# Banded attention and a two-projection feed-forward net on one core: the operands of both projections moved to fixed places modulo 128 bytes

## The chip, the cores and the metric

The kernel runs on one core of one Trainium2 chip. The metric is the device time of one execution in microseconds (us); lower is better. Three executions of the kernel before took 661.93, 663.27 and 664.57 us, so the median is 663.27 us.

## The reference: what is computed

Eight heads of attention over four sequences of 768 positions with head size 64, with a linear bias by distance and a mask that keeps a band of 96 positions and 8 global ones, and behind it a net with one hidden layer of 2048 and a leaky gate, on 3072 rows of 512.

```python
# q, k, v: (4, 8, 768, 64)
scores = q @ k.T / 8 + bias            # bias = -slope[head] * distance
scores = where(is_global | is_local, scores, -1e9)   # n_global = 8, n_local = 96
a = softmax(scores)
x = (a @ v) as rows of 8 * 64          # 3072 x 512
h = x @ w_in                           # 512 x 2048
g = maximum(0.01 * h, h)
out = g @ w_out                        # 2048 x 512
```

## The kernel before

**Two paths.** `fast_path` computes all under the assumption that the band holds (few global positions, a short band). At the end `band_holds` (line 756) looks whether it did, and only if not a general path (`general_attention`, `general_ffn`) computes everything again. With the inputs here the general path is skipped.

**Work units.** The 3072 rows are 24 steps of 128 rows. The attention of a step is two units of four heads, so there are 48 units, each handled in an "event" (line 348): scores (line 192), biased scores on VectorE (line 206), exponentials on ScalarE (line 219), sums, a transposition (by TensorE for the first 14 units, line 278, by VectorE and DMA for the others, lines 250 and 223), the product with v (line 324), and a split of the resulting x into a rounded part `xh` and a rest `xl` (lines 345 and 346).

**The projections.** To keep float32 precision, each operand is kept as two fp32r tiles, a rounded high part and a low rest (`wih`/`wil` for w_in, `woh`/`wol` for w_out, `xh`/`xl`, `gh`/`gl`), and each product is three matmuls: high by high, high by low, low by high. In the first projection the weights are stationary and x moves (lines 891 to 893 for the first two chunks of 384 rows, line 449 for the nine chunks of 256 rows); in the second one the gated hidden values `gh`/`gl` are stationary and the weights move, 512 wide (lines 912 to 914, and line 493). The text below calls a run of first-projection matmuls an **H group** (24 matmuls of 256 columns at line 449; 12 of 384 before that) and a run of the second an **O group** (12 matmuls of 512 columns, 9 of them in the early part).

**Eight pairs to a chunk.** A chunk of 256 rows goes through eight pairs of hidden blocks, `p` = 0 to 7. In each step `s` of the last loop (line 631) stand first the attention events that are due, then the H group of step `s`, its gate (line 453), and the O group of step `s - 2`. Eight of the nine such chunks multiply the last three pairs (`p` = 5, 6, 7) with seven products instead of eight half products, from precomputed sums of weight blocks (`prepare`, line 537, tiles `h5` to `h7` and `l5` to `l7`); such an O group has 21 matmuls, nearly all 256 columns wide; in pair 5 two of them are 512 wide. `prepare` also overwrites a quarter of `woh` and `wol` for these pairs (line 568).

**Order.** TensorE's matmuls are kept in the order of the program, and nearly all of ScalarE's and VectorE's instructions too.

**Where tiles lie.** Tiles are placed in pools one behind the other, so that the size of a tile shifts all later ones in its pool and in the pools behind it, while pools with `side="right"` are placed from the other end of the memory and do not shift. The pool `keep` (line 922) holds the weights; behind it come `const`, `raw` (q, k, v), `att`, and then `ffn`, `kept_rows` and `x0`, which are given back to be used by `a` (`gh`, `gl`), `ev` and `w` (`h5` ...). The pools `x1`, `x2` (`xh`, `xl` of the later chunks), `t` and `pt` (`pt_d`) are on the right side. A tile `gap` of 16 floats ahead of the sums in `prepare` (line 542) already shifts these by 64 bytes.

Of the kernel before, what the change touches and what calls it, by code (L numbers as in the profile page):

```python
# [10 lines left out]
F32 = mybir.dt.float32  # L11
F32R = mybir.dt.float32r
BF16 = mybir.dt.bfloat16
I32 = mybir.dt.int32
I64 = mybir.dt.int64
# [3 lines left out]
P = 128  # L19
# [13 lines left out]
FAST = 3  # L33
# [18 lines left out]
def fast_path(ctx, tc, qp, kp, vp, wi, wo, nvec, weights, nmall, out, B, H, S):  # L52
    nc = tc.nc
    NB = S // P
    DM = H * D
    NK = DM // P
    NF = wi.shape[0]
# [7 lines left out]
    wih, wil, woh, wol = weights  # L65
# [5 lines left out]
    ffn = later.enter_context(tc.tile_pool(name="ffn", bufs=2))  # L71
    kept_rows = later.enter_context(tc.tile_pool(name="kept_rows", bufs=1))
    xts = {0: later.enter_context(tc.tile_pool(name="x0", bufs=1))}
    edge = ctx.enter_context(tc.tile_pool(name="edge", bufs=1, side="right")).tile([P, EDGE], F32, name="edge")
    nc.gpsimd.memset(edge, 0.0)
    stage = early.enter_context(tc.tile_pool(name="stage", bufs=STAGES, side="right"))
# [572 lines left out]
def split_float64(tc, pin, pool, raw, dh, dl):  # L649

    nc = tc.nc
    w2 = raw.bitcast(I32).rearrange("p (n two) -> p n two", two=2)
    lo, hi = w2[:, :, 0], w2[:, :, 1]
    w = pool.tile([P, lo.shape[1]], F32, tag="work", name="w32", bufs=2)
    wb = w.bitcast(I32)
    w3 = w.rearrange("p (a b) -> p a b", a=dh.shape[1]) if len(dh.shape) == 3 else w

    def scale():  # L660
        pin(nc.scalar.activation(out=w, in_=hi.bitcast(F32), func=AF.Copy, scale=2.0 ** -112))

    def shift():
        pin(nc.vector.tensor_scalar(out=wb, in0=wb, scalar1=3, scalar2=0x7FFFFFF8,
                                    op0=ALU.logical_shift_left, op1=ALU.bitwise_and))
        pin(nc.vector.scalar_tensor_tensor(out=wb, in0=hi, scalar=-0x80000000, in1=wb,
                                           op0=ALU.bitwise_and, op1=ALU.bitwise_or))

    def low():
        pin(nc.vector.scalar_tensor_tensor(out=wb, in0=lo, scalar=29, in1=wb,  # L670
                                           op0=ALU.logical_shift_right, op1=ALU.bitwise_or))

    def high():
        pin(nc.scalar.copy(out=dh, in_=w3))

    def rest():
        pin(nc.vector.tensor_tensor(out=dl, in0=w3, in1=dh.bitcast(F32), op=ALU.subtract))

    return scale, shift, low, high, rest
# [172 lines left out]
                    nc.sync.dma_start(out=dst.rearrange("o d s -> (o d) s"), in_=xo)  # L852


def general_ffn(tc, weights, xs, out):
    nc = tc.nc
    wih, wil, woh, wol = weights
    NK, NF, DM = wih.shape[1], woh.shape[1], woh.shape[2]
    CT = xs.shape[-1]
    with ExitStack() as ctx:  # L860
        work = ctx.enter_context(tc.tile_pool(name="hwork", bufs=2))
        ps_h = ctx.enter_context(tc.tile_pool(name="hps", bufs=2, space=bass.MemoryType.PSUM))
        ps_o = ctx.enter_context(tc.tile_pool(name="hpo", bufs=1, space=bass.MemoryType.PSUM))
        xv = xs.rearrange("b j p k t -> (b j) p k t")
        ov = out.rearrange("(c p) m -> c p m", p=CT)
        with tc.For_i(0, xv.shape[0], 1) as c:
            x = work.tile([P, NK, CT], F32, name="hx", bufs=1)
            xh = work.tile([P, NK, CT], F32R, name="hxh", bufs=1)
            xl = work.tile([P, NK, CT], F32R, name="hxl", bufs=1)
            nc.sync.dma_start(out=x, in_=xv[bass.ds(c, 1)].rearrange("o p k t -> (o p) k t"))  # L870
            nc.scalar.copy(out=xh, in_=x)
            nc.vector.tensor_tensor(out=xl, in0=x, in1=xh.bitcast(F32), op=ALU.subtract)
            o = ps_o.tile([P, CT // P, DM], F32, name="hpo")
            for f in range(NF):
                gh, gl = hidden(tc, lambda ins: None, work, ps_h, weights, xh, xl, f, CT)
                for tt in range(CT // P):
                    project(tc, o[:, tt, :], weights, gh, gl, tt, f, f == 0, f == NF - 1)
            ob = work.tile([P, CT // P, DM], F32, name="hob")
            nc.scalar.copy(out=ob, in_=o)
            nc.sync.dma_start(out=ov[bass.ds(c, 1)].rearrange("o (t p) m -> p (o t) m", p=P), in_=ob)  # L880


def hidden(tc, pin, pool, psum, weights, xh, xl, f, CT, *steps):

    nc = tc.nc
    wih, wil = weights[:2]
    NK = wih.shape[1]
    fs = slice(f * P, (f + 1) * P)
    ps = psum.tile([P, CT], F32, tag="ps_h", name="ps_h")
    for k in range(NK):  # L890
        tc.keep_in_program_order(nc.tensor.matmul(ps, lhsT=wih[:, k, fs], rhs=xh[:, k, :CT], start=(k == 0), stop=False))
        tc.keep_in_program_order(nc.tensor.matmul(ps, lhsT=wih[:, k, fs], rhs=xl[:, k, :CT], start=False, stop=False))
        tc.keep_in_program_order(nc.tensor.matmul(ps, lhsT=wil[:, k, fs], rhs=xh[:, k, :CT], start=False, stop=(k == NK - 1)))
    t = pool.tile([P, CT], F32, name="t")
    pin(nc.scalar.copy(out=t, in_=ps))
    pin(nc.vector.scalar_tensor_tensor(out=t, in0=t, scalar=0.01, in1=t, op0=ALU.mult, op1=ALU.max))
    gh = pool.tile([P, CT], F32R, name="gh")
    gl = pool.tile([P, CT], F32R, name="gl")
    if steps:
        steps[0]()  # L900
    pin(nc.scalar.copy(out=gh, in_=t))
    pin(nc.vector.tensor_tensor(out=gl, in0=t, in1=gh.bitcast(F32), op=ALU.subtract))
    if steps:
        steps[1]()
    return gh, gl
# [11 lines left out]
def tile_kernel(tc, a, out, B, H, S):  # L917
    nc = tc.nc
    NF, _, NK, _ = a["wi"].shape
    DM = a["wo"].shape[3]  # L920
    NB = S // P
    with tc.tile_pool(name="keep", bufs=1) as keep, tc.tile_pool(name="xs", bufs=1, space=bass.MemoryType.DRAM) as dram:
        nvec = read_counts(tc, keep, a["ngl"])
        nmall = keep.tile([P, B * NB * H], F32, name="nmall")
        weights = (keep.tile([P, NK, NF * P], F32R, name="wih"), keep.tile([P, NK, NF * P], F32R, name="wil"),
                   keep.tile([P, NF, DM], F32R, name="woh"), keep.tile([P, NF, DM], F32R, name="wol"))
        fast_path(tc, a["qp"], a["kp"], a["vp"], a["wi"], a["wo"], nvec, weights, nmall, out, B, H, S)
        with tc.tile_pool(name="fin", bufs=1) as fin:
            flag = nc.values_load(band_holds(tc, fin, nvec, nmall), min_val=0, max_val=1,  # L929
                                  skip_runtime_bounds_check_because="the flag is a product of comparisons")  # L930
        with tc.If(flag == 0):
            xs = dram.tile([B, S // 256, P, NK, 256], F32, name="xs")
            general_attention(tc, a["qt"], a["kt"], a["vt"], nvec, xs, B, H, S)
            general_ffn(tc, weights, xs, out)


def layout(q, k, v, wi, wo, ng, nl):
# [47 lines left out]
```

## Time and profile before

| | |
|---|---|
| median of three runs | 663.27 us (661.93 to 664.57) |
| profiled execution | 659.95 us, its span 658.2 us |
| mean granted TensorE clock | 0.988 |
| TensorE matmul busy (PE) | 626.5 us, 95% of the span, 6275 instructions |
| weight loads (PEld) | 557.0 us, 85% |
| VectorE (DVE) | 423.9 us, 64% |
| ScalarE (ACT) | 294.9 us, 45% |
| GpSimd (POOL) | 82.3 us, 13% |
| DMA | 79.76 MB, 121 GB/s on average |

The page gives for every engine its busy time; TensorE's matmuls are pipelined, the recorded end of one lies behind the start of the next, so the pace of a stream of matmuls is read from the distance of their starts in the timeline, not from their durations. PEld, the loading of the next stationary operand, runs beside the matmul before it. A row of the view of groups reads: line, engine, operation, out<-in, shapes, count | busy time in us, mean ns of one | idle time before, and what ended it.

### The profile page before, as it was taken

To read this page: it belongs to the slowest core of one execution; us is meant where nothing else is said; L and a number is where in the kernel's file an instruction comes from. 1 tells how busy PE (TensorE), PEld (TensorE's weight loads), DVE (VectorE), ACT (ScalarE), POOL (GpSimd) and SP (SyncE) were. 2 spreads that over 40 slices of the span, in tenths; PEclk is the share of its full clock that TensorE was granted. 3 is DMA by queue.
4 is the path that set the end of the run, shared out by engine and by line. 5 is a ranking of instruction groups with operands and counts; after the bars stand their busy time and mean duration, and the time that the engine had idled before them with its cause. 6 is when DMAs were issued, how large, how long until landed. Compare 5 with 4: busy or idle time off the path is not lost. (4 is left out here: it accounts for less than half of the span.)

```text
span 658.2 us, 15933 instructions
## 1 busy us (share of the span) xinstructions
PE 626.5 (95%) x6275; PEld 557.0 (85%) x6275; DVE 423.9 (64%) x1210; ACT 294.9 (45%) x770; POOL 82.3 (13%) x148
## 2 busy tenths in 40 slices
PE   5779999999999999899999999999999999999994
PEld 4568889999888888789889889889889889889893
DVE  5979988886657437957556656656755756534443
ACT  5877755554434424535334434334334434322221
POOL 3444700000101101001001001001001001100000
PEclk9789999999999999999999999999999999999998
DMA  8776643322546425224433433523432532300001
GB/s 280 239 243 183 210 131 126 122 77 79 159 147 217 144 64 172 76 77 138 151 98 107 167 114 88 157 87 113 153 116 80 170 115 58 116 1 1 33 1 37
DMA packets 52098, 79.76 MB, mean 121 GB/s; under 512 B 7728, under 2 KB 27184, under 8 KB 52016
## 3 DMA queue, kind: packets, MB, share of 16 engines
q1 hardware_dynamic: 52016, 78.67, 37.7%
q8 instruction: 51, 0.84, 0.5%
q14 instruction: 31, 0.25, 0.1%
HBM read 59.51 MB, written 19.14 MB: 119 GB/s over the span
## 5 line engine op out<-in xcount | busy, mean ns | idle before, releaser
L468 ACT CAST gh<-t 128x512 fp32r<-128x512 f32 (+1 forms) x72 | 52.4, 727 | 134.5 <-PE ps_p L493 80.1
L469 DVE TENSOR_TENSOR gl<-t,gh 128x512 fp32r<-128x512 f32 (+1 forms) x72 | 59.3, 824 | 68.3 <-ACT gh L468 62.9
L219 ACT ACTIVATE pr<-pr,nmall 128x192 f32<-128x192 f32 (+1 forms) x192 | 83.3, 436 | 18.7 <-DVE nmall L206 18.7
L461 DVE SCALAR_TENSOR_TENSOR t<-t 128x512 f32<-128x512 f32 x72 | 49.5, 688 | 59.9 <-ACT t L460 59.4
L449 PE MATMUL ps_p<-xh,wih 128*128 128x256 f32 x288 | 82.4, 286 | 0.0
L449 PE MATMUL ps_h<-xh,wih 128*128 128x256 f32 x288 | 80.9, 281 | 0.0
L449 PE MATMUL ps_h<-xl,wih 128*128 128x256 f32 x288 | 80.0, 278 | 0.0
L449 PE MATMUL ps_h<-xh,wil 128*128 128x256 f32 x288 | 79.9, 277 | 0.0
L449 PE MATMUL ps_p<-xl,wih 128*128 128x256 f32 x288 | 79.9, 277 | 0.0
L449 PE MATMUL ps_p<-xh,wil 128*128 128x256 f32 x288 | 79.8, 277 | 0.0
L48 POOL TENSOR_SCALAR xh<-x 128x256 fp32r<-128x256 f32 x48 | 21.8, 454 | 452.1 <-ACT x L330 370.5
L449 PEld LDWEIGHTS ps_p<-xh,wih 128*128 128x128 f32 x288 | 54.1, 188 | 6.3 <-issue 5.7
L493 PE MATMUL ps_m<-woh,gl 128*128 128x512 f32 (+1 forms) x168 | 58.0, 345 | 0.0
L493 PE MATMUL ps_m<-wol,gh 128*128 128x512 f32 (+1 forms) x168 | 57.7, 343 | 0.0
L493 PE MATMUL ps_m<-woh,gh 128*128 128x512 f32 (+1 forms) x168 | 57.7, 343 | 0.0
L449 PEld LDWEIGHTS ps_h<-xh,wih 128*128 128x128 f32 x288 | 54.2, 188 | 3.0 <-issue 2.2
L206 DVE CUSTOM_DVE_ANT_0 pr<-ps_av,nbw 128x192 f32<-128x192 f32 x136 | 40.5, 354 | 23.7 <-ACT x L330 23.5
L449 PEld LDWEIGHTS ps_h<-xl,wih 128*128 128x128 f32 x288 | 54.1, 188 | 0.8
L449 PEld LDWEIGHTS ps_p<-xl,wih 128*128 128x128 f32 x288 | 54.1, 188 | 0.5
L449 PEld LDWEIGHTS ps_h<-xh,wil 128*128 128x128 f32 x288 | 54.1, 188 | 0.0
L449 PEld LDWEIGHTS ps_p<-xh,wil 128*128 128x128 f32 x288 | 54.1, 188 | 0.0
L493 PE MATMUL ps_p<-woh,gh 128*128 128x512 f32 (+1 forms) x120 | 46.3, 385 | 3.1 <-ACT t L460 2.3
(133 smaller groups left out, 1478.4 us busy)
## 6 DMA issues: line engine op xcount, KB each, us to landing
via<-pr SPq DMA_DIRECT2D x30, 384.0 KB, 2.5
pt_d<-via SPq DMA_DIRECT2D x120, 96.0 KB, 2.4
kr<-in_kp_dram SPq DMA_DIRECT2D x40, 256.0 KB, 3.6
vr<-in_vp_dram SPq DMA_DIRECT2D x40, 256.0 KB, 3.4
wst<-in_wi_dram SPq DMA_DIRECT2D x16, 512.0 KB, 3.6
wst<-in_wo_dram SPq DMA_DIRECT2D x16, 512.0 KB, 3.5
qs<-in_qp_dram SPq DMA_DIRECT2D x24, 256.0 KB, 3.7
out_dram<-part SPq DMA_DIRECT2D x21, 256.0 KB, 2.5
```

The costliest lines, as they stand in the source:

```text
L48: return eng.tensor_scalar(out=dst, in0=src, scalar1=1.0, scalar2=1.0, op0=ALU.mult, op1=ALU.mult)
L206: pin(nc.vector.tensor_tensor_reduce(out=head(u, pr, a, j), in0=own(u, ps[:, j, a * KW:(a + 1) * KW]), in1=nb, scale=-0.125, scalar=3.0e38 ...
L219: pin(nc.scalar.activation(out=p, in_=p, func=AF.Exp, scale=-1.0, bias=nm[:, 2 * a + j:2 * a + j + 1], accum_out=sm[:, 2 * a + j:2 * a + j ...
L449: tc.keep_in_program_order(nc.tensor.matmul(o, lhsT=w[:, k, fs], rhs=x[:, k, :], start=(k + i == 0), stop=(k == NK - 1 and i == 2)))
L461: pin(nc.vector.scalar_tensor_tensor(out=g, in0=g, scalar=0.01, in1=g, op0=ALU.mult, op1=ALU.max))
L468: pin(nc.scalar.copy(out=gh[:, :n - a0], in_=t[:, a0:n]))
L469: pin(nc.vector.tensor_tensor(out=gl[:, :n - a0], in0=t[:, a0:n], in1=gh[:, :n - a0].bitcast(F32), op=ALU.subtract))
L493: tc.keep_in_program_order(nc.tensor.matmul(to, lhsT=x[:, a], rhs=y, start=first and n == 0, stop=last and n == 2))
```

## The change

The change allots three unused tiles of 64 bytes and moves no computation. The first stands between `wil` and `woh` in `keep`, the second ahead of `xh` and `xl` of the first chunk in pool `x0`, each cleared once on GpSimd so that it counts as used; `prepare` keeps its own. Everything that is placed behind the first gap on the left side moves up by 64 bytes, the x tiles of the first chunk by 128; the right side stays. From the built program, the start of each operand modulo 128 bytes (matmuls of the fast path, all columns and blocks of one operand have the same remainder):

| matmul | moving, before | stationary, before | moving, after | stationary, after |
|---|---|---|---|---|
| first projection, lines 449, 891 to 893 | `xh`, `xl`: 64 | `wih`, `wil`: 0 | 64 | 0 |
| second projection, lines 493, 912 to 914 | `woh`, `wol`, `h`, `l`: 0 | `gh`, `gl`: 64 | 64 | 0 |
| scores, line 192 | `kr`: 0 | `qs`: 0 | 64 | 64 |
| transposition, line 278 | `dg`: 64 | `pr`: 0 | 0 | 64 |
| product with v, units 0 to 13, line 324 | `pt`: 64 | `vr`: 0 | 0 | 64 |
| product with v, later units, line 324 | `pt_d`: 64 | `vr`: 0 | 64 | 64 |

In the general path, which is skipped here, the three pairs of blocks of `woh` and `wol` that `prepare` overwrites are loaded and converted again before they are used.

```diff
@@ fast_path
     xts = {0: later.enter_context(tc.tile_pool(name="x0", bufs=1))}
+    nc.gpsimd.memset(xts[0].tile([P, 16], F32, tag="gap", name="gap"), 0.0)
     edge = ctx.enter_context(tc.tile_pool(name="edge", bufs=1, side="right")).tile([P, EDGE], F32, name="edge")
@@ general_ffn
-def general_ffn(tc, weights, xs, out):
+def general_ffn(tc, weights, wo, xs, out):
...
+        for f in range(NF - 2 * FAST, NF, 2):
+            t = work.tile([P, DM], I64, name="hst")
+            nc.sync.dma_start(out=t, in_=wo[f].rearrange("p a b -> p (a b)"))
+            for step in split_float64(tc, lambda ins: None, work, t, woh[:, f], wol[:, f]):
+                step()
@@ tile_kernel
-        weights = (keep.tile([P, NK, NF * P], F32R, name="wih"), keep.tile([P, NK, NF * P], F32R, name="wil"),
-                   keep.tile([P, NF, DM], F32R, name="woh"), keep.tile([P, NF, DM], F32R, name="wol"))
+        wih, wil = (keep.tile([P, NK, NF * P], F32R, name=name) for name in ("wih", "wil"))
+        nc.gpsimd.memset(keep.tile([P, 16], F32, name="gap"), 0.0)
+        woh, wol = (keep.tile([P, NF, DM], F32R, name=name) for name in ("woh", "wol"))
+        weights = wih, wil, woh, wol
...
-            general_ffn(tc, weights, xs, out)
+            general_ffn(tc, weights, a["wo"], xs, out)
```

On the fast path the only place at which an engine's order of instructions differs is GpSimd's beginning; on the four other engines each instruction stands where it stood. GpSimd before, from its first own memset on (`edge` is a small tile of zeros, `ident` the identity matrix with which TensorE is warmed up, `loc` and `col` are tables of positions for the bias):

```order
L75 MEMSET edge 128x8
masks.py:197 MEMSET ident 128x128
L696 ISA
L696 IOTA loc 128x256
L699 IOTA col 128x64
masks.py:199 AFFINE_SELECT ident<-ident 128x128
```

GpSimd now, at the same place (line numbers behind the edits are larger by one to eight):

```order
L932 MEMSET gap 128x16
L74 MEMSET gap 128x16
L76 MEMSET edge 128x8
masks.py:197 MEMSET ident 128x128
L697 ISA
L697 IOTA loc 128x256
L700 IOTA col 128x64
masks.py:199 AFFINE_SELECT ident<-ident 128x128
```

Two memsets of 16 columns have come to stand ahead of `edge`, and `ident`, `loc` and `col` follow them in their old order.

## Prediction

> **What bounds the kernel now.** I read the page first, then the busy time by stretches, the groups by form, and the timeline of TensorE, where the starts of its matmuls are to be seen.
>
> ```profile
> PE 626.5 (95%) x6275; PEld 557.0 (85%) x6275; DVE 423.9 (64%) x1210; ACT 294.9 (45%) x770; POOL 82.3 (13%) x148
> PE   5779999999999999899999999999999999999994
> ```
>
> ```profile
> 42.00:160.00 118.00, 116.31 (x1044) 104.48 (x1036) 101.23 (x211) 70.90 (x165) 22.65 (x35) 0.99 0.42 131
> 200.00:641.00 441.00, 437.92 (x4133) 390.44 (x4132) 262.41 (x773) 172.28 (x443) 36.47 (x64) 1.00 0.33 104
> ```
>
> The columns of the second fence are the stretch, its length, and the busy time of PE, PEld, DVE, ACT and POOL, then the granted clock. From 200 to 641 us TensorE is busy for 437.92 of 441 us at full clock, and the next engine, VectorE, for 262.41. So the kernel is bound by the pace at which TensorE takes matmuls, and the question is only whether this pace depends on where operands lie. The timeline shows the pace. Here are an O group of 21 matmuls of 256 columns (from 601.71), the H group behind it (from 604.09) and the first matmul of the next O group.
>
> ```profile
> 601.59 0.28 PE L449 MATMUL ps_h<-xh,wil 128*128 128x256 f32 x1
> 601.71 0.28 PE L493 MATMUL ps_m<-h,gh 128*128 128x256 f32 x1
> ...
> 603.97 0.28 PE L493 MATMUL ps_m<-woh,gl 128*128 128x256 f32 x1
> 604.09 0.28 PE L449 MATMUL ps_p<-xh,wih 128*128 128x256 f32 x1
> ...
> 606.80 0.28 PE L449 MATMUL ps_p<-xh,wil 128*128 128x256 f32 x1
> 606.92 0.28 PE L493 MATMUL ps_m<-h,gh 128*128 128x256 f32 x1
> ```
>
> The first 21 matmuls take 2.38 us, 113.3 ns each; the next 24, of the same width, take 2.83 us, 117.9 ns each. There are two rhythms, 4.6 ns apart, each kept for a whole group. I call them fast and slow. The fast one is found with weights that move from 0 and stationary values at 64 (the O group), and in most H groups with the opposite places; both projections know both rhythms. The 512-wide matmuls have two as well (first rows of one group, last rows of another):
>
> ```profile
> 326.75 0.39 PE L493 MATMUL ps_m<-woh,gh 128*128 128x512 f32 x1
> ...
> 329.26 0.40 PE L493 MATMUL ps_p<-woh,gl 128*128 128x512 f32 x1
> ```
>
> ```profile
> 364.36 0.40 PE L493 MATMUL ps_m<-woh,gh 128*128 128x512 f32 x1
> ...
> 366.93 0.39 PE L493 MATMUL ps_p<-woh,gl 128*128 128x512 f32 x1
> ```
>
> Eleven distances in each: 2.51 us (228.2 ns) in the fast, 2.57 us (233.6 ns) in the slow one, 5.4 ns apart.
>
> **The change part by part. Inside a group: 0.** In the second projection, moving and stationary operand both go up by 64 bytes, so their distance is the same as before to the byte; in the first projection neither moves, but for the first chunk. Before as after, one of the two lies at 64 and one at 0. A pace that hangs on how the two streams meet can't change by this within a group. Of the first chunk, whose x moves by 128 bytes, I take the same, as it stays at 64.
>
> **At the hand-over between groups: -0.35 us, from -3.4 to +4.6.** What does change is the load of the first stationary block of a group, which runs beside the last matmul of the group before. In the program before, H hands to O with moving x at 64 and stationary gh at 64; O hands to H with both at 0. Afterwards they differ there too. The price of such a like pair is in the fence above: the matmul at 601.59, beside which gh is loaded, takes 0.12 us to the next start, and those at 603.97 and 606.80 also 0.12 us, as inside. So the like pair costs nothing itself. But behind O groups of 512 wide matmuls the H group starts unevenly:
>
> ```profile
> 323.77 0.39 PE L493 MATMUL ps_p<-woh,gl 128*128 128x512 f32 x1
> 324.00 0.28 PE L449 MATMUL ps_h<-xh,wih 128*128 128x256 f32 x1
> ...
> 324.59 0.28 PE L449 MATMUL ps_h<-xh,wil 128*128 128x256 f32 x1
> ```
>
> Five distances take 0.59 us where the fast rhythm has 0.567, so 0.023 us are lost, in 30 direct hand-overs of this kind, the first and the last being these:
>
> ```profile
> 220.06 0.28 PE L449 MATMUL ps_h<-xh,wih 128*128 128x256 f32 x1
> ...
> 637.50 0.28 PE L449 MATMUL ps_p<-xh,wih 128*128 128x256 f32 x1
> ```
>
> That is 0.7 us in all. It may come from the like pair (then it goes) or from the change of width (then it stays): 0 to -0.7, and having no row that parts these, I take the middle, -0.35. The other thing at stake at a hand-over is which rhythm the next group falls into. I followed all groups: 9 of 71 H groups are slow (first at 298.97, last at 604.09), 15 of 24 O groups of 21 (first at 295.03, last at 640.24), 4 of 48 O groups of 12 (the first is the one at 364.36 above).
>
> ```profile
> 298.97 0.38 PE L449 MATMUL ps_h<-xh,wih 128*128 128x256 f32 x1
> ...
> 640.24 0.39 PE L493 MATMUL ps_m<-h,gh 128*128 128x512 f32 x1
> ```
>
> If all of them became fast, that is 9 x 24 x 4.6 ns = 1.0 us, 15 x 21 x 4.6 ns = 1.4 us and 4 x 12 x 5.4 ns = 0.3 us, with the 0.7 us above 3.4 us in all. Some hand-overs turn a fast run slow (the one at 604.09) and others a slow one fast; without the like pair a group would more likely keep the rhythm it finds, which helps where it is fast and hurts where it is slow. I take 0 for this, between the two rivals below.
>
> **GpSimd's two memsets: 0.** Their place is here:
>
> ```profile
> 0.31 0.10 POOL L975 MEMSET const-bfloat16-1.0<- 128x1 bf16 x1
> 0.35 0.10 POOL L975 MEMSET const-uint8-127<- 128x1 uint8 x1
> 0.74 0.10 POOL L75 MEMSET edge<- 128x8 f32 x1 [0.29 <-POOLq L975]
> ...
> 1.79 2.50 PE L262 MATMUL ps_w<-ident 128*128 128x128 f32 x10 [1.79 <-POOL ident masks.py:199]
> ...
> 5.06 1.13 PE L192 MATMUL ps_sc<-kr,qs 64*64 64x128 f32 x16 [0.76 <-DMA kr<-in_kp_dram]
> ```
>
> One of this kind takes 0.10 us and a next one starts 0.04 us later, so the identity comes 0.08 to 0.2 us later and with it the ten warming matmuls. They end at 4.29 us, and what follows waits for the keys until 5.06; 0.77 us of cover. Without it the cost would be 0.2 us. Behind these memsets GpSimd has the tables `loc` and `col`, which VectorE takes up only after the counts have landed.
>
> **Attention: 0, up to +1.4 us.** Here two relations change: the product with v of the later units gets a like pair (64 and 64), and the scores keep theirs. What a like pair costs in these narrow matmuls is in today's scores:
>
> ```profile
> L192 PE MATMUL ps_av<-kr,qs 64*64 64x192 f32 x544 | 28.6, 325 | 0.0
> L324 PE MATMUL ps_av<-pt_d,vr 64*64 64x128 f32 x512 | 21.9, 282 | 0.0
> L324 PE MATMUL ps_av<-pt_d,vr 64*64 64x64 f32 x512 | 13.5, 217 | 0.0
> ```
>
> From 64 to 128 columns, at unlike places, a matmul gets longer by 65 ns; from there to the 192 columns of the scores, at like places, by another 43. Nothing says that the like pair is slower. Were it slower by the share that parts the rhythms, 4% of 21.9 + 13.5 us, it would cost 1.4 us. I take 0, the nearer row.
>
> **Waits behind a faster TensorE.** One wait is fixed by ScalarE, not by the matmuls ahead of it:
>
> ```profile
> PEld ps_p L493 <- ACT t L460: 11.7, 20, 2.8
> ```
>
> In 20 O groups the fourth matmul waits for ScalarE's copy out of the same PSUM tile; whatever the three matmuls ahead of it gain there is lost again. They are 60 of some 880, so I leave it out.
>
> **The sum.** On the profiled execution (span 658.2 us, with 1.75 us around it 659.95 us) it is -0.35 us. This execution lies 3.3 us below the median of the runs shown; I take the difference over as it is: 663.27 - 0.35 = 662.9 us.
>
> A rule of the Trainium skill speaks for no effect at all: SBUF — State Buffer, section "Who interferes with whom", says that TensorE never waits on anyone and has two independent read ports, one for each operand; by it the sum is 0 and the time 663.3 us. The trace bears it out only in part, since the same instructions run at 113.3 and at 117.9 ns, so something makes them wait.
>
> **The rivals.**
>
> *Faster.* Unlike places all through keep TensorE in the fast rhythm: -3.4 us. The 512-wide matmuls could at best cost what two of 256 do, 226.6 against 228.2 ns, and 880 of them give another 1.4 us. The end is 663.3 - 4.8 = 658.5 us. For it speaks that the fast O group at 601.71 hands to a slow H group with a like pair. Against it: the slow group at 295.03 has unlike places from its first to its last matmul.
>
> *Slower.* The other end is this same row, as a mechanism:
>
> ```profile
> 295.03 0.39 PE L493 MATMUL ps_m<-h,gh 128*128 128x512 f32 x1
> 295.26 0.28 PE L493 MATMUL ps_m<-l,gh 128*128 128x256 f32 x1
> ...
> 295.85 0.40 PE L493 MATMUL ps_m<-h,gh 128*128 128x512 f32 x1
> ```
>
> This group begins with one 512-wide matmul and goes on with 256-wide ones at unlike places, and it is slow at once: five in 0.59 us, 118 ns. Hand-over from 512 to 256 columns without the like pair is what the change makes of the 30 direct hand-overs from O to H, which today end in the fast rhythm after five matmuls. If they do as this group, each costs 24 x 4.6 ns less the 0.023 us, so 0.087 us, and the O group behind it 12 x 5.4 ns = 0.065 us: 0.15 us, 4.6 us for all 30, and 667.9 us. It decides the sign as soon as three of them fall so, and is over 0.5% from 22 on.
>
> *No effect on the pace.* If the starts of H groups come only from the change of width, nothing moves: 663.3 us. This lies within my forecast's band.
>
> **How the numbers follow.** About 0.5%, 3.3 us, is what a measurement of this kernel can tell from no change. The forecast and the rival without effect are both inside it: together 0.62. The slower rival gets 0.20, since a row shows its rhythm at the very kind of hand-over that the change makes; the faster one 0.18, since it needs both the rhythm and a pace at 512 columns that no row shows. The range is 658.5 us, the end of the faster rival, to 668.5, the end of the slower one with half of the attention's bound.
>
> **What would show it.** In the new profile, the distance of starts inside groups should still be 113.3 or 117.9 ns, and 228 or 234; the number of slow groups near 9, 15 and 4. H groups behind O groups of 512 columns that start evenly at 113 ns show the -0.7 us; ones that run at 118 ns to their end show the slower rival. A third rhythm, or another distance of the scores or of the product with v, would make the reasoning wrong: then the place itself counts, not the relation of the two operands.

## The result, and the profile after

Six executions of the changed kernel took 664.40 to 667.47 us, median 665.93; six of the kernel before, the three shown ahead of the prediction among them, 659.81 to 664.57 us, median 661.38. The ratio on record, which is not simply the quotient of these two medians, is 1.0061, with a 95% interval of 1.0033 to 1.009: slower by some 4 us. The forecast was 662.9 us and no measurable change; the time lies inside the range, on the side of the slower rival.

The profiled execution took 665.92 us, its span is 664.1 us (658.2 before). The page's line of busy times, engine by engine:

```profile
PE 630.9 (95%) x6275; PEld 560.7 (84%) x6275; DVE 424.1 (64%) x1210; ACT 295.0 (44%) x770; POOL 82.7 (12%) x150
```

Only TensorE's busy time has grown, PE by 4.4 us and PEld by 3.7, with the same 6275 instructions. VectorE and ScalarE work as long as before, and GpSimd has its two memsets more. So the loss is to be looked for in the pace of the matmuls rather than in new waits. The timeline of TensorE shows where. This is the H group that the prediction showed at 324.00 (L450 is now the first projection, L494 the second), the last matmul of the O group ahead of it and the O group behind it:

```profile
326.70 0.39 PE L494 MATMUL ps_p<-woh,gl 128*128 128x512 f32 x1
326.93 0.28 PE L450 MATMUL ps_h<-xh,wih 128*128 128x256 f32 x1
...
327.51 0.28 PE L450 MATMUL ps_h<-xh,wil 128*128 128x256 f32 x1
...
329.63 0.28 PE L450 MATMUL ps_h<-xh,wil 128*128 128x256 f32 x1
329.75 0.40 PE L494 MATMUL ps_m<-woh,gh 128*128 128x512 f32 x1
...
330.69 0.39 PE L494 MATMUL ps_p<-wol,gh 128*128 128x512 f32 x1
...
332.28 0.40 PE L494 MATMUL ps_p<-woh,gl 128*128 128x512 f32 x1
```

Before, the first five distances were uneven (0.59 us) and the rest fast: from 324.00 to 326.75, 2.75 us to the next O group. Now the first five are 0.58 us, and the slow rhythm stays: 326.93 to 329.75, 2.82 us, 117.5 ns a matmul. The O group behind it begins with four distances in 0.94 us (some 235 ns) and then finds back to seven in 1.59 us (some 228 ns, as before). So it is in all 30 H groups that directly follow an O group of 512 columns; the first and the last:

```profile
222.05 0.28 PE L450 MATMUL ps_h<-xh,wih 128*128 128x256 f32 x1
...
224.88 0.40 PE L494 MATMUL ps_m<-woh,gh 128*128 128x512 f32 x1
...
637.87 0.28 PE L450 MATMUL ps_h<-xh,wih 128*128 128x256 f32 x1
...
640.70 0.40 PE L494 MATMUL ps_m<-woh,gh 128*128 128x512 f32 x1
```

Both take 2.83 us by these rows, 24 times some 118 ns. Two more kinds of groups changed. The O group of 21 that stood at 601.71, fast with 2.38 us, is now slow with 2.47:

```profile
607.14 0.28 PE L494 MATMUL ps_m<-h,gh 128*128 128x256 f32 x1
...
609.61 0.28 PE L450 MATMUL ps_p<-xh,wih 128*128 128x256 f32 x1
```

And H groups behind an attention event are slow more often. The same one before and after, from its first matmul to the next O group (2.84 us, then 2.93):

```profile
265.81 0.38 PE L449 MATMUL ps_p<-xh,wih 128*128 128x256 f32 x1
...
268.65 0.39 PE L493 MATMUL ps_m<-woh,gh 128*128 128x512 f32 x1
```

```profile
268.46 0.39 PE L450 MATMUL ps_p<-xh,wih 128*128 128x256 f32 x1
...
271.39 0.40 PE L494 MATMUL ps_m<-woh,gh 128*128 128x512 f32 x1
```

Followed through all groups of the two profiled executions, the slow ones are:

| groups | before | after |
|---|---|---|
| H behind an O group of 512 columns, 30 | 0 | 30 |
| H behind attention, 32 | 4 | 19 |
| H behind an O group of 21, 9 | 5 | 3 |
| O groups of 21, 24 | 15 | 24 |
| O groups of 12, 48 | 4 slow throughout | none throughout; all begin slow and recover |

To put one number on this I add up, over all matmuls of both projections that wait for nothing, by how much the distance to the next start is above 113.3 ns (256 columns), 173.3 ns (384) or 228.9 ns (512); a shorter distance counts as negative. This **lost pace** is 4.3 us before and 9.2 us after: +3.4 us in the H groups, +0.8 in the 256-wide matmuls of the O groups, +0.5 in the 512-wide ones, and +0.1 in the 384-wide ones. Its growth of 4.8 us covers what the runs differ by (4 us) and leaves 1.1 us of the two spans' 5.9 open. The first H group of 256 columns starts 1.67 us later than before (199.12 us where it was 197.45), and 1.5 us of this is there at 47 us already, in the opening stretch, where TensorE is busy for some 25 of the first 42 us only. Nothing shows that this belongs to the change: over all profiled executions of this document that group starts between 196.8 and 200.0 us, and with e10 below, whose time is that of the kernel before, it is 198.89.

The other terms came out as written. GpSimd's beginning:

```profile
0.74 0.11 POOL L932 MEMSET gap<- 128x16 f32 x1 [0.29 <-POOLq L983]
0.79 0.11 POOL L74 MEMSET gap<- 128x16 f32 x1
0.83 0.10 POOL L76 MEMSET edge<- 128x8 f32 x1
...
1.88 2.51 PE L263 MATMUL ps_w<-ident 128*128 128x128 f32 x10 [1.88 <-POOL ident masks.py:199]
...
5.19 1.13 PE L193 MATMUL ps_sc<-kr,qs 64*64 64x128 f32 x16 [0.81 <-DMA kr<-in_kp_dram]
```

The warming matmuls start 0.09 us later than before, and the first scores still wait 0.81 us for the keys: covered. The groups of attention, and the wait behind ScalarE:

```profile
L193 PE MATMUL ps_av<-kr,qs 64*64 64x192 f32 x544 | 29.2, 329 | 0.0
L325 PE MATMUL ps_av<-pt_d,vr 64*64 64x128 f32 x512 | 22.0, 282 | 0.0
L325 PE MATMUL ps_av<-pt_d,vr 64*64 64x64 f32 x512 | 13.6, 217 | 0.0
```

```profile
PEld ps_p L494 <- ACT t L461: 11.4, 20, 2.6
```

The product with v, whose pair is now like modulo 128, takes 282 and 217 ns as before; the wait has 11.4 us instead of 11.7. The scores' mean goes from 325 to 329 ns, but from 190 us on it is 323.1 ns before and after; the difference lies in the first 60 us, and e10 has the 329 too.

### The profile page after: what moved, and what is told of

Same layout as the page of the kernel before. It is cut to its first block, busy times and chain, and to the rows that moved or that the text cites. A ratio compares the mean times of both kernels' runs of the same rounds, so it can differ in the third digit from the quotient of the medians.

```text
span 664.1 us, 15935 instructions
## 1 busy us (share of the span) xinstructions
PE 630.9 (95%) x6275; PEld 560.7 (84%) x6275; DVE 424.1 (64%) x1210; ACT 295.0 (44%) x770; POOL 82.7 (12%) x150
## 5 line engine op out<-in xcount | busy, mean ns | idle before, releaser
L450 PE MATMUL ps_p<-xh,wih 128*128 128x256 f32 x288 | 83.2, 289 | 0.0
L450 PE MATMUL ps_h<-xh,wih 128*128 128x256 f32 x288 | 81.4, 282 | 0.0
L450 PE MATMUL ps_p<-xh,wil 128*128 128x256 f32 x288 | 80.6, 280 | 0.0
L450 PE MATMUL ps_p<-xl,wih 128*128 128x256 f32 x288 | 80.6, 280 | 0.0
L450 PE MATMUL ps_h<-xh,wil 128*128 128x256 f32 x288 | 80.5, 280 | 0.0
L450 PE MATMUL ps_h<-xl,wih 128*128 128x256 f32 x288 | 80.5, 279 | 0.0
L450 PEld LDWEIGHTS ps_p<-xh,wih 128*128 128x128 f32 x288 | 54.1, 188 | 6.2 <-issue 5.7
L494 PE MATMUL ps_m<-woh,gh 128*128 128x512 f32 (+1 forms) x168 | 58.1, 346 | 0.0
L494 PE MATMUL ps_m<-woh,gl 128*128 128x512 f32 (+1 forms) x168 | 57.8, 344 | 0.0
L494 PE MATMUL ps_m<-wol,gh 128*128 128x512 f32 (+1 forms) x168 | 57.8, 344 | 0.0
L450 PEld LDWEIGHTS ps_h<-xh,wih 128*128 128x128 f32 x288 | 54.0, 188 | 3.0 <-issue 2.2
L450 PEld LDWEIGHTS ps_p<-xh,wil 128*128 128x128 f32 x288 | 54.9, 191 | 0.0
L450 PEld LDWEIGHTS ps_h<-xh,wil 128*128 128x128 f32 x288 | 54.8, 190 | 0.0
L450 PEld LDWEIGHTS ps_h<-xl,wih 128*128 128x128 f32 x288 | 54.1, 188 | 0.8
L450 PEld LDWEIGHTS ps_p<-xl,wih 128*128 128x128 f32 x288 | 54.1, 188 | 0.5
L494 PE MATMUL ps_p<-woh,gh 128*128 128x512 f32 (+1 forms) x120 | 46.7, 389 | 2.7 <-ACT t L461 2.2
```

The costliest lines, as they stand in the source:

```text
L450: tc.keep_in_program_order(nc.tensor.matmul(o, lhsT=w[:, k, fs], rhs=x[:, k, :], start=(k + i == 0), stop=(k == NK - 1 and i == 2)))
L494: tc.keep_in_program_order(nc.tensor.matmul(to, lhsT=x[:, a], rhs=y, start=first and n == 0, stop=last and n == 2))
```

## The experiments

All move operands only, by unused tiles or by smaller scratch tiles; apart from the clearing of the unused tiles, order and work stay. In the expectations and from here on, places count modulo 256 bytes where that is said, and the **distance** of a pair is the place of the stationary operand less that of the moving one. Modulo 256, the kernel before has x at 192, w_in at 0, w_out at 0, gh and gl at 192: distance 64 in H, 192 in O. After the change w_out is at 64 and gh, gl at 0: the distances are the same (but for the x of the first chunk, which goes from 64 to 192), but from group to group the places stand 64 apart where they stood 0 apart (gh against x, w_in against w_out). Every count of slow groups and every pace is of one profiled execution of a kernel, while times and ratios are of all its executions; the profiled one can lie off the median (e2's took 663.48 us, 2.7 less).

**First batch: modulo 128.** In the first run (e1) attention's operands were meant to lie as after the change, and the projections to stay:

```diff
+    nc.gpsimd.memset(ctx.enter_context(tc.tile_pool(name="gapa", bufs=1)).tile([P, 16], F32, name="gapa"), 0.0)
     raw = ctx.enter_context(tc.tile_pool(name="raw", bufs=2))
...
+    nc.gpsimd.memset(ctx.enter_context(tc.tile_pool(name="gapb", bufs=1)).tile([P, 16], F32, name="gapb"), 0.0)
     ffn = later.enter_context(tc.tile_pool(name="ffn", bufs=2))
+    nc.gpsimd.memset(later.enter_context(tc.tile_pool(name="gapk", bufs=1)).tile([P, 16], F32, name="gapk"), 0.0)
...
+    nc.gpsimd.memset(xts[0].tile([P, 16], F32, name="gapx"), 0.0)
```

> The kernel before, with attention alone at the places of the changed kernel (scores 64 and 64, product with v 64 and 64 for the later units, the early units swapped); both projections as before. Theory of the hand-over: H groups are made slow by the load of w_in's first block beside the last matmul of an O group whose weights lie at another place modulo 128; that hand-over is as before here, so about 9 of 71 H groups run at 117.8 ns and the ratio to before is 1.000 (within 0.002). Rival, attention: what stands between the groups sets the rhythm; then H groups behind attention run at 117.8 ns as in the changed kernel (19 of 32 instead of 4), some 1.6 us and a ratio of 1.002 to 1.003. Rival, place of the second projection: 1.000.

Measured: 665.43 us, ratio 1.0046 (1.0024 to 1.0069). But the timeline says that this was not attention alone. gh and gl had moved by 128 bytes, which modulo 128 is nothing, and the 512-wide matmuls now took another pace (first and last of an O group of 12):

```profile
330.30 0.39 PE L497 MATMUL ps_m<-woh,gh 128*128 128x512 f32 x1
...
332.86 0.39 PE L497 MATMUL ps_p<-woh,gl 128*128 128x512 f32 x1
```

2.56 us for eleven distances, 232.7 ns, in nearly all O groups of 12, where before 44 of 48 were fast at 228 to 229. So modulo 128 is too coarse for a place, I count modulo 256 from here on, and the run says nothing on attention. The second run (e2) has the same flaw: w_out up by 64, and gapa, gapb and gapk as in e1, which were meant to bring attention back to its old places.

```diff
-        weights = (keep.tile([P, NK, NF * P], F32R, name="wih"), keep.tile([P, NK, NF * P], F32R, name="wil"),
-                   keep.tile([P, NF, DM], F32R, name="woh"), keep.tile([P, NF, DM], F32R, name="wol"))
+        wih, wil = (keep.tile([P, NK, NF * P], F32R, name=name) for name in ("wih", "wil"))
+        nc.gpsimd.memset(keep.tile([P, 16], F32, name="gap1"), 0.0)
+        woh, wol = (keep.tile([P, NF, DM], F32R, name=name) for name in ("woh", "wol"))
+        weights = wih, wil, woh, wol
```

> The changed kernel, with attention alone put back to its places of before. Theory of the hand-over: all 30 H groups behind an O group of 512-wide matmuls stay slow (117.8 ns), ratio to before 1.005 to 1.007. Rival, attention: the H groups behind attention are fast again, and if these carry the others, all are; ratio 1.000 to 1.002. Rival, place of the second projection (moving at 64, stationary at 0): slow as in the changed kernel, 1.005 to 1.007.

Measured: 666.15 us, 1.0056 (1.0037 to 1.0076); 34 of 71 H groups slow, 12 of the 30 behind 512 columns, the 512-wide matmuls again at 232 to 234 ns. Third (e3), all operands of the projections on each other's places, with a gap of 64 bytes ahead of w_in, of w_out, of the first x, and on the right side of x1 and x2:

```diff
+    nc.gpsimd.memset(xts[0].tile([P, 16], F32, name="gapx"), 0.0)
...
+    nc.gpsimd.memset(early.enter_context(tc.tile_pool(name="gapr", bufs=1, side="right")).tile([P, 16], F32, name="gapr"), 0.0)
     xts[1] = early.enter_context(tc.tile_pool(name="x1", bufs=1, side="right"))
...
+            nc.gpsimd.memset(ctx.enter_context(tc.tile_pool(name="gaps", bufs=1, side="right")).tile([P, 16], F32, name="gaps"), 0.0)
             xts[STD] = ctx.enter_context(tc.tile_pool(name="x2", bufs=4, side="right"))
...
+        nc.gpsimd.memset(keep.tile([P, 16], F32, name="gap0"), 0.0)
+        wih, wil = (keep.tile([P, NK, NF * P], F32R, name=name) for name in ("wih", "wil"))
+        nc.gpsimd.memset(keep.tile([P, 16], F32, name="gap1"), 0.0)
```

> All moving operands of both projections at 0 and all stationary ones at 64, so unlike places everywhere as in the changed kernel but with the second projection at its places of before and the first one moved; attention as before. Theory of the hand-over: only the relation counts, so the 30 H groups behind 512-wide O groups are slow, ratio 1.005 to 1.007. Rival, place of the second projection: its operands lie as before, so the H groups are fast, 9 of 71 slow, ratio 1.000.

Measured: 663.47 us, 1.0031 (1.0012 to 1.005), with 61 of 71 H groups slow (24 of the 30) and a lost pace of 8.9 us; the time lies between the two that were expected. Fourth (e5), a like pair inside O and none from H to O: gapb and gapk as in e1, and the gap in `prepare` left out.

```diff
-            gap = late["w"].tile([P, 16], F32, tag="gap", name="gap")
-            nc.gpsimd.memset(gap, 0.0)
```

> The kernel before with gh and gl (and the sums h, l) at 0: the first projection unlike (64 and 0), the second one alike (0 and 0), hand-over from H to O unlike, from O to H alike as before. Theory of the hand-over: the H groups behind O groups stay fast (113.3 ns) as before, since the place of w_out against w_in is as before; the like pair inside O groups shows its own price there: if a like pair costs what parts the rhythms, 512-wide matmuls take 233.6 instead of 228.2 ns, 880 of them 4.8 us, ratio 1.007, otherwise 1.000. Rival, place of the second projection (its moving operand at 64 makes it slow): H fast and O unchanged, 1.000.

Measured: 662.67 us, 1.002 (1.0002 to 1.0038). 18 of the 30 are slow, where they were expected to stay fast; the 512-wide matmuls run at 226.6 to 228.1 ns over a whole group, the 256-wide ones of the O groups of 21 at 119 to 120, a pace not seen before.

**Second batch: the change taken apart, modulo 256.** To shift one set of operands by 64 and leave the others, the sum of the gaps is brought to a multiple of 256, or a scratch tile is made smaller by as much. The second projection alone (e7):

```diff
+    nc.gpsimd.memset(ctx.enter_context(tc.tile_pool(name="gapb", bufs=1)).tile([P, 16], F32, name="gapb"), 0.0)
     ffn = later.enter_context(tc.tile_pool(name="ffn", bufs=2))
+    nc.gpsimd.memset(later.enter_context(tc.tile_pool(name="gapk", bufs=1)).tile([P, 48], F32, name="gapk"), 0.0)
...
-    one = const.tile([P, 32], F32, name="one")[:, :1]
+    one = const.tile([P, 16], F32, name="one")[:, :1]
...
+        nc.gpsimd.memset(keep.tile([P, 16], F32, name="gap1"), 0.0)
```

> The operands of the second projection (w_out's two parts, gh, gl, and the h and l of the converted blocks) lie 64 bytes higher modulo 256, as after the change; attention's operands and the x of every chunk lie where they lay before it. Theory 1 (the hand-over from a 512-wide O group to an H group decides, by the distance of the two groups' operands): 665 to 666.3 us against 661.7, at least 25 of the 30 H groups behind O groups of 512 columns slow to their end, and H groups behind attention near 4 of 32. Theory 2 (attention's own places make the loss): 661.2 to 662.4 us, the 30 groups fast as before. If both have a part: 663 to 665.

Measured: 665.68 us, 1.0044 (1.0025 to 1.0062), 30 of the 30 slow, lost pace 9.6 us. The same H group as above, 2.82 us:

```profile
326.99 0.28 PE L451 MATMUL ps_h<-xh,wih 128*128 128x256 f32 x1
...
329.81 0.40 PE L495 MATMUL ps_m<-woh,gh 128*128 128x512 f32 x1
```

As far as the intervals tell, this is the whole cost of the change. One thing is unlike theory 1: of the H groups behind attention 18 of 32 are slow, though neither they nor attention moved. Attention alone (e10):

```diff
+    nc.gpsimd.memset(ctx.enter_context(tc.tile_pool(name="gapa", bufs=1)).tile([P, 16], F32, name="gapa"), 0.0)
     raw = ctx.enter_context(tc.tile_pool(name="raw", bufs=2))
...
-        rs = att.tile([P, 16], F32, name="rs")[:, :4]
+        rs = att.tile([P, 8], F32, name="rs")[:, :4]
```

> Attention's operands (the two of the scores, v and the mask's) alone lie 64 bytes higher, as after the change; both projections' operands lie where they lay before it, modulo 256. Theory 1: H groups behind O groups of 512 columns stay fast (at most 3 of 30 slow); at most the 32 behind attention change, up to 19 of them slow, each 0.1 us: 661.5 to 663.3 us. Theory 2 (attention makes the loss): 664.5 us or more.

Measured: 661.60 us, 0.999 (0.9971 to 1.0009), 0 of the 30 slow, 5 of 32 behind attention, lost pace 4.4 us: the kernel before. The same H group takes 2.75 us again:

```profile
325.88 0.28 PE L450 MATMUL ps_h<-xh,wih 128*128 128x256 f32 x1
...
328.63 0.39 PE L494 MATMUL ps_m<-woh,gh 128*128 128x512 f32 x1
```

Next, the second projection higher by 128 (e8) and by 192 (e9), with x and, but for 128 bytes, attention as before:

```diff
+    nc.gpsimd.memset(later.enter_context(tc.tile_pool(name="gapk", bufs=1)).tile([P, 32], F32, name="gapk"), 0.0)
...
+        nc.gpsimd.memset(keep.tile([P, 32], F32, name="gap1"), 0.0)
```

> The operands of the second projection lie 128 bytes higher than before the change; x as before; attention's operands 128 higher. Rival (places count modulo 128, as the prediction had it): nothing moves, 661.2 to 662.4 us, slow H groups near 9 of 71. Theory 1 with places counted modulo 256: the distance between the groups is new, so the pattern of slow groups is not that of before: over 20 slow H groups of 71 or a new pace, 663 us or more.

Measured: 664.41 us, 1.0034 (1.0018 to 1.005); 18 of the 30 and 31 of all 71 slow.

```diff
+    nc.gpsimd.memset(ctx.enter_context(tc.tile_pool(name="gapb", bufs=1)).tile([P, 16], F32, name="gapb"), 0.0)
     ffn = later.enter_context(tc.tile_pool(name="ffn", bufs=2))
+    nc.gpsimd.memset(later.enter_context(tc.tile_pool(name="gapk", bufs=1)).tile([P, 16], F32, name="gapk"), 0.0)
...
-    one = const.tile([P, 32], F32, name="one")[:, :1]
+    one = const.tile([P, 16], F32, name="one")[:, :1]
...
+        nc.gpsimd.memset(keep.tile([P, 48], F32, name="gap1"), 0.0)
```

> The operands of the second projection lie 192 bytes higher than before the change; x as before; attention's operands 128 higher. Rival (modulo 128): the same as the changed kernel, 665 to 666.5 us with the 30 H groups behind O groups of 512 columns slow. Theory 1 modulo 256: a distance of its own, with a number of slow H groups other than 52 of 71; the theory does not say which way, between 661 and 666.5 us.

Measured: 661.66 us, 0.9994 (0.9979 to 1.001); 1 of the 30 and 11 of 71 slow, lost pace 4.4 us. Modulo 128 the first of these is the kernel before and the second the changed one; both did the opposite of what that says. The count modulo 128, on which the change and my tables went, is too coarse.

**Third batch: distances or places.** All of both projections higher by 64 (e11), so that the second one lies just where the change has it; three scratch tiles of attention (`one`, `sm`, `rs`) are cut to 8 floats to make room:

```diff
+    nc.gpsimd.memset(early.enter_context(tc.tile_pool(name="gapr", bufs=1, side="right")).tile([P, 48], F32, name="gapr"), 0.0)
...
-    one = const.tile([P, 32], F32, name="one")[:, :1]
+    one = const.tile([P, 8], F32, name="one")[:, :1]
...
+            nc.gpsimd.memset(ctx.enter_context(tc.tile_pool(name="gaps", bufs=1, side="right")).tile([P, 48], F32, name="gaps"), 0.0)
...
+        nc.gpsimd.memset(keep.tile([P, 16], F32, name="gap0"), 0.0)
+        wih, wil = (keep.tile([P, NK, NF * P], F32R, name=name) for name in ("wih", "wil"))
```

> All operands of both projections (x, w_in, w_out, gh, gl, h, l) lie 64 bytes higher modulo 256 than before the change, so the second projection lies exactly where the changed kernel has it, and every distance between operands is that of before. Attention's operands lie 32 lower. Theory 1 (distances between the operands decide): 661 to 662.6 us and at most 5 of the 30 H groups behind O groups of 512 columns slow. Rival (the places of the second projection by themselves decide, whatever the first one's are): 665 us or more and at least 25 of the 30 slow.

Measured: 661.11 us, 0.9987 (0.9972 to 1.0001), 3 of the 30 slow; the same H group takes 2.75 us:

```profile
326.64 0.28 PE L450 MATMUL ps_h<-xh,wih 128*128 128x256 f32 x1
...
329.39 0.39 PE L494 MATMUL ps_m<-woh,gh 128*128 128x512 f32 x1
```

So it is the places of the two projections against each other, not the second one's by themselves. Then w_out alone 64 lower (e12), which is 192 higher, and what lies behind w_out brought back by smaller tiles `one`, `sm` and `rs` and a gap of 8 floats:

```diff
+        nc.gpsimd.memset(keep.tile([P, 48], F32, name="gap1"), 0.0)
```

> The two parts of w_out alone lie 64 bytes lower modulo 256 than before the change, so at the place of their stationary operands gh and gl (in an earlier run such 512-wide matmuls took some 227.5 ns instead of 229); x, w_in, gh, gl, h and l as before, attention 128 higher. Theory 1, with the distances counted modulo 256: from O to H the distance is that of the run with the second projection 192 bytes higher, from H to O that of before, both of which left the groups behind 512 columns fast; with 880 x 1.5 ns = 1.3 us less at 512 columns, 659.8 to 661.5 us. Rival (what the first hand-over run with like places in O showed, 18 of 30 slow, comes from the like places themselves): 662 to 663.5 us.

Measured: 663.97 us, 1.0037 (1.0023 to 1.0052); 26 of the 30 slow. This was forecast wrong: the two distances between the groups had each been harmless in an earlier run, but together, and with distance 0 in O, they are not; the rival, that like places in O make H groups slow, comes nearer. Nor did the 512-wide matmuls gain anything:

```profile
327.32 0.40 PE L494 MATMUL ps_m<-woh,gh 128*128 128x512 f32 x1
...
328.71 0.39 PE L494 MATMUL ps_m<-woh,gh 128*128 128x512 f32 x1
...
329.84 0.39 PE L494 MATMUL ps_p<-woh,gl 128*128 128x512 f32 x1
```

The first six distances take 1.39 us (some 232 ns), and only the last five, in 1.13 us, keep some 226.5 ns. All eleven take 229.1 to 229.3 ns a distance in the O groups of 12 without a wait, where most of these took 228.7 to 228.8 in the kernel before. The O groups of 21 are at 118.6 to 120 ns. Then w_in and w_out both 64 lower (e13), and w_in alone (e14), for which gap1 of 16 floats is added to the gap0 shown (in both, scratch tiles behind it are smaller again):

```diff
+        nc.gpsimd.memset(keep.tile([P, 48], F32, name="gap0"), 0.0)
```

> Moving and stationary operands of both projections all lie at one place modulo 256 (w_in and w_out 64 bytes lower than before the change), except h and l of the converted blocks, which stay 64 above their stationary operand; attention 128 higher. If 256-wide matmuls at one place take the 120 ns that the O groups of pairs showed in the run with like places, the 1728 of the H groups cost 6 ns each more: 671 to 674 us. If the 120 ns came from the changes of width there, the H groups run at 113.3 or below and the 512-wide ones at 227.5: 658.5 to 661 us.

> The two parts of w_in alone lie 64 bytes lower modulo 256, so at the place of x; x and the second projection lie as before the change; attention 96 lower. Theory 1: from O to H the distance is that of the changed kernel, from H to O that of before; if the first decides, at least 25 of the 30 H groups behind O groups of 512 columns run at their slower pace to the end, if the second decides, at most 5. In the first case some 4 us more than before, 665 to 666.5, in the second 661 to 662.5; and should 256-wide matmuls at one place cost 120 ns, 671 us or more and no two rhythms.

Measured: 671.31 us, 1.0135 (1.0109 to 1.0161), and 671.65 us, 1.0159 (1.0131 to 1.0186). In both, all 71 H groups run at 119 to 120 ns and none has a faster rhythm. The same group in the first of them, 2.87 us:

```profile
330.42 0.28 PE L450 MATMUL ps_h<-xh,wih 128*128 128x256 f32 x1
...
333.29 0.40 PE L494 MATMUL ps_m<-woh,gh 128*128 128x512 f32 x1
```

At one place a 256-wide matmul of an H group costs 119 to 120 ns and the fast rhythm is gone. The rule of the Trainium skill that the prediction cited (SBUF — State Buffer, section "Who interferes with whom": two independent read ports, and TensorE waits on no one) does not cover this: only places of operands moved, and the runs are 9 us and more slower.

**Fourth batch: is there a distance with the fast rhythm alone?** x of the H groups 64 lower, so at distance 128 from w_in, in the kernel before (e15) and in the changed one (e18):

```diff
+            nc.gpsimd.memset(ctx.enter_context(tc.tile_pool(name="gaps", bufs=1, side="right")).tile([P, 16], F32, name="gaps"), 0.0)
             xts[STD] = ctx.enter_context(tc.tile_pool(name="x2", bufs=4, side="right"))
```

> Only the x of the H groups lies 64 bytes lower than before the change, 128 modulo 256 from w_in (all else as before). Theory A (the two rhythms belong to the distances 64 and 192; at 128 there is only the faster one): no H group of 71 at 117.8 ns to its end, the 2.2 us that H groups spend above 113.3 ns go, 659 to 660.5 us. Theory B (two rhythms at every distance but zero, and the hand-over picks): between 5 and 60 slow H groups of 71 at 117 to 118 ns, 661 to 666 us. Between them: one pace of its own, under 113 or over 118 ns.

Measured: 668.83 us, 1.0103 (1.0089 to 1.0117). No rhythm of 113.3 at all: the 71 groups take 118.3 to 120.0 ns a distance, most of them 118.3 to 118.9, and their distances are uneven throughout, from 112 to 124 ns. The same group, 2.83 us:

```profile
327.36 0.28 PE L449 MATMUL ps_h<-xh,wih 128*128 128x256 f32 x1
...
330.19 0.40 PE L493 MATMUL ps_m<-woh,gh 128*128 128x512 f32 x1
```

> The changed kernel with only the x of the H groups 64 bytes lower, 128 modulo 256 from w_in. Theory A: all 30 H groups behind O groups of 512 columns are fast though the second projection lies where the change put it; H groups spend 5.6 us less than in the changed kernel, 660 to 661.5 us, some 4.5 below the changed kernel. Theory B: many of the 30 stay slow, 663 to 666.5 us.

Measured: 669.51 us, 1.0116 (1.01 to 1.0131), 118.3 to 119.8 ns. Theory A, and with it the hope for a faster kernel, falls, and theory B too: at 128 there is neither rhythm, but an uneven pace of its own, slower than both. Then w_out 64 higher, at distance 128 from gh and gl (e16), and with the x of e15 as well (e17):

```diff
-    one = const.tile([P, 32], F32, name="one")[:, :1]
+    one = const.tile([P, 16], F32, name="one")[:, :1]
...
+        nc.gpsimd.memset(keep.tile([P, 16], F32, name="gap1"), 0.0)
```

> Only the two parts of w_out lie 64 bytes higher than before the change, 128 modulo 256 from gh and gl. The 512-wide matmuls were seen at some 227.5, 233 and 229 ns at distances 0, 64 and 192; at 128 I expect them between: 227.5 to 233, so -1.3 to +3.5 us over the 880 of them. Theory A does not say which rhythm the H groups take, whose own distance stays 64: the first matmul behind the O group decides. 660.5 to 667 us.

Measured: 665.41 us, 1.0052 (1.0038 to 1.0066). 30 of the 30 slow, as in the changed kernel; the 512-wide matmuls at 231.6 to 233.0 ns over a whole group.

> w_out as in the run before (128 from gh and gl) and the x of the H groups 128 from w_in. Theory A: no slow H group, -2.2 us on the H groups, and the 512-wide matmuls as in the run before: 658 to 660.5 us if these are no slower than 229 ns, the fastest kernel of all. Theory B: slow H groups remain, 661 to 667 us.

Measured: 671.07 us, 1.0139 (1.0121 to 1.0157). Both theories forecast less. The ratio is about that of the two moves one behind the other (1.0103 and 1.0052), though the H groups that e16 had slow can't be so a second time.

All runs side by side, the lost pace against the time:

| run | distance in H, in O | slow of the 30 | lost pace, us | ratio to before |
|---|---|---|---|---|
| before | 64, 192 | 0 | 4.3 | 1 |
| attention alone (e10) | 64, 192 | 0 | 4.4 | 0.999 |
| second up 192 (e9) | 64, 192 | 1 | 4.4 | 0.9994 |
| all up 64 (e11) | 64, 192 | 3 | 5.1 | 0.9987 |
| second up 128 (e8) | 64, 192 | 18 | 8.5 | 1.0034 |
| second up 64 (e7) | 64, 192 | 30 | 9.6 | 1.0044 |
| the change | 64, 192 | 30 | 9.2 | 1.0061 |
| e5 | 64, 0 | 18 | 6.0 | 1.002 |
| e12 | 64, 0 | 26 | 8.4 | 1.0037 |
| e1 | 64, 64 | 13 | 8.3 | 1.0046 |
| e2 | 64, 64 | 12 | 9.0 | 1.0056 |
| e16 | 64, 128 | 30 | 10.3 | 1.0052 |
| e3 | 192, 192 | 24 | 8.9 | 1.0031 |
| e15 | 128, 192 | other pace | 12.5 | 1.0103 |
| e18 | 128, 192 | other pace | 12.8 | 1.0116 |
| e17 | 128, 128 | other pace | 14.6 | 1.0139 |
| e13 | 0, 0 | other pace | 15.8 | 1.0135 |
| e14 | 0, 192 | other pace | 16.2 | 1.0159 |

A line through the kernel before gives 0.8 us of time for each us of lost pace, with a correlation of 0.98 over the table; why it is not a full us is not shown. The first seven rows have the same distances inside both projections; they differ in where the two lie against each other (and in attention and first x), and hold both the fastest kernels and the changed one.

## Why the prediction was wrong

**"Inside a group: 0" held.** The H groups still know 113.3 and some 118 ns and nothing else.

**The step that failed is the hand-over**, the sentence "I take 0 for this, between the two rivals below" on the rhythm into which the next group falls, and with it the -0.35 us. The prediction had seen that only the pairs from group to group change, and the slower rival named what happens there: H groups behind 512 columns slow to their end. All 30 were, where I had forecast none in particular. e7 shows that this comes from moving the second projection alone, e11 that it goes when the first moves along. By the rival's price these H groups are 30 x 0.087 = 2.6 us, and the one shown grew by 0.07 us (2.75 to 2.82; 0.079 in the mean of the 30), so 2.4 us: the mechanism at about its price. Its other half was too dear: the O groups behind are slow for four matmuls, not twelve, and the 512-wide ones lost 0.5 us in all instead of 30 x 0.065 = 2.0. In exchange two things came that neither sum held: 15 more slow H groups behind attention, about 0.09 us each, 1.4 us, and nine more slow O groups of 21, 0.8 us.

**What led me there.** I read "the like pair costs nothing itself" from three distances of 0.12 us, in which 113 and 118 ns cannot be told apart. And I took the step from two rows of other hand-overs: the fast O group at 601.71 (256 to 256 columns) for harmless, the slow one at 295.03 (512 to 256) as a mere rival, though the change's 30 hand-overs are of the second kind. The row at 295.03 was the nearer one, and it is not alone: before the change all eight O groups of 21 that begin with a 512-wide matmul are slow.

**The number hides part of the miss.** The forecast of 662.9 us stood on a base of 663.27 us from three executions; with six it is 661.38. So the time is 3.0 us above the forecast, but the change is some 4 us where -0.35 was forecast. That the time still lies inside the stated range says that the range reached to the end of the slower rival, not that the reasoning held.

**The settle** of five uneven distances, 0.7 us in 30 groups, did not go: where an H group is slow it has no settle to lose, since it stays slow to its end.

**The count modulo 128** did no harm inside the sum, but it would have on the next step: e8 and e9 are wrong by it in both directions.

**GpSimd, attention and the wait behind ScalarE** were 0 as written; for attention e10 shows it (0.999, 0.9971 to 1.0009).

**What stays open.** Which hand-over ends in which rhythm follows no rule that I found: with the distances inside the groups unchanged, a shift of the second projection by 0, 64, 128 and 192 leaves 0, 30, 18 and 1 of the 30 slow, but e12 was forecast wrong from the two distances. And in e7 the H groups behind attention change although they, attention, and the 32 or 48 matmuls of attention in between lie where they lay. What stands ahead of attention goes with this: behind an O group of 12 and 48 matmuls of attention, 0 of 16 H groups are slow before, 16 of 16 after the change and 15 of 16 in e7; behind an O group of 21 and 48 matmuls, 0 of 8 in all three. This speaks for an effect of the O group that reaches across attention; how it does so was not tried. No version beat both kernels: e11, e9 and e10 cannot be told from the kernel before.

## What to carry to other kernels

Where one engine is busy for 95% of the span, its pace is a term of the sum like any other, and a change of memory places alone moves it: here by up to 1.6%. Read the pace from the distance of starts over whole groups, and follow every group: in the kernels before and after, each H group keeps to its end the rhythm that it shows behind its first few matmuls. Moving a set of buffers without those that are used next to it changes the hand-over even when every pair inside stays as it was, and what lies behind it in the pool moves too, as in e1 and e2.

## What the runs showed of the hardware

The pace of a 256-wide fp32r matmul hangs on the distance of its two operands in a partition. In the H groups of these runs, with places counted modulo 256 bytes, it is 119 to 120 ns at 0 (e13, e14), 118.3 to 120.0 at 128 (e15, e18), and at 64 and 192 either 113.3 or some 118 (the kernels before and after, e3). That 128 is too short a period is shown by e8 and e9; a shift by 256 alone was not tried.

A 512-wide one takes, over a whole O group of 12 without a wait, 226.6 to 228.1 ns (e5) or 229.1 to 229.3 (e12, e13) at 0, where it settles at 226.7 in all three, 232.5 to 233.6 at 64 (e1, e2), 231.6 to 233.5 at 128 (e16, e17), and 228.6 to 230.8 or some 233.5 at 192. So the distance at which 512 columns settle fastest is one at which 256 columns have no fast rhythm. I had expected neither that places count beyond modulo 128 nor that like places help one width and hurt the other.
